# Chunked attention and a leaky-ReLU layer pair on one core: block 4's first layer in seven products, and a new order of the steps

## The chip, the cores and the metric

The kernel runs on one core of a Trainium2 chip (trn2). The metric is the device time of one execution in microseconds; of several runs the median is taken. All inputs and the output lie in HBM as fp32; the kernel computes in fp16 with fp32 sums.

## The reference

```python
# attention in chunks of 64 positions: q, k, v are (8 batches, 8 heads, 576, 64)
scores = scale * q_c @ k_c^T;  scores -= max(scores)
attn = exp(scores);  attn /= sum(attn) + 1e-9
out = attn @ v_c
# the heads side by side: x is (4608 tokens, 512)
h = x @ w_in                 # w_in  (512, 2048)
g = maximum(0.01 * h, h)
return g @ w_out             # w_out (2048, 512)
```

## The kernel before, in words

The 4608 tokens are worked through in two units. Attention goes by 36 groups of 128 tokens (two chunks of 64 for each of 8 heads); the two layers go by 19 blocks, two of 128 tokens and 17 of 256 (`BLOCKS`, line 46). Block j from 2 on consists of groups 2j-2 and 2j-1. All is in SBUF once; x of a group goes to a ring of 12 groups (`xT`, line 90).

The code emits one step after another from a list written out by hand, `ORDER` (lines 588 to 678). A step's name gives its function (`STAGES`, line 679) and its numbers; an apostrophe (`other=1`) sends it to another engine. Each engine runs its own steps in the order of the list and waits on semaphores for what it reads or overwrites. A second string, `BANKS` (line 60), names, for each tile in the order in which the steps ask for one, the PSUM bank (8 of them) or the buffer of a small ring that it gets. A tile in a bank can begin when all readers of the tile before it there are done.

For group u the steps are: `g` loads q and k (two DMAs, or four, issued by POOL), `tq`, `tk` transpose on TensorE (PE) into PSUM, with `q`, `k` copying out, or, from group 14 on, `tdq`, `tdk` transpose by a DMA issued by SP, with `cq` copying q into its padded place; `s` is the scores (8 matmuls of 64 columns), `m` the maximum and `b` the subtraction (DVE), `x` the exponential (ACT), `z` three small steps up to 1/sum, `n` the product with it (DVE, or POOL with an apostrophe), then either `e`, `c` (transpose on PE, copy) or `d` (DMA transpose from SP); `v` multiplies with v (8 matmuls of 64 columns), `a` copies x into `xT`. `L` and `vl` load v of a batch on POOL.

The layers have plain and seven-product (Strassen-like) forms.

- First layer, plain (`mm1`, line 361, step `M`): a step is 16 matmuls of 128 columns into one bank (in halves of 128 tokens, p = 1, 2, for blocks 2 to 4), and `act1` (line 386, step `G`) is the leaky ReLU on ACT from that bank to the hidden tile `gT`.
- First layer in seven products (`wide`, line 420, step `V`), from block 5 on: tokens, inputs and outputs are halved, and for each of two parts s of the outputs seven steps of 8 matmuls of 128 columns go into three banks (`xbank`, `xz`, `seed`). It needs differences of `w_in` (`w_in_sum`, line 399, step `WS`, on DVE, once), four sums of x per block (`x_sums`, line 406, step `xs`, DVE or POOL), a copy of the first product to a second bank (`wide_seed`, line 451, `ls`), a copy of the fifth to SBUF (`wide_five`, line 455, `lf`), two additions per part on DVE (`wide_add`, line 459, `la`) and four leaky ReLUs per part (`wide_leaky`, line 463, `lp`).
- Second layer: blocks 0 and 1 plain (`mm2`, line 567, step `B`, four matmuls of 512 columns, and `plain_out`, step `O`); from block 2 on seven products (`product`, line 504, step `R`, 8 matmuls of 256 columns) of sums of `gT` (`token_sums`, line 490, step `sum`, DVE) and of `w_out` (`weight_sum`, line 477, step `W`), put together by `combine` (line 551, step `comb`): 1, 6, 7 copy a partial result to SBUF, 2, 3, 5 add two into the output tile, 4 copies into it, 0 adds product 5 to a kept one.

`LATE` (line 47) lists blocks whose token halves change places in the second layer. `FIVE` (line 49) lists blocks in which products 3 and 5 have a bank each, `Z3` and `Z5`, and need `comb.0`; in the others product 3 goes on top of product 5 in one bank. `store` (line 582) writes an output tile from SP's queue. Output tiles of blocks 0 to 3 share a ring of six with the copies of `lf`; later ones have a ring of four.

## Time and profile before

| what | us |
|---|---|
| median of 3 runs (275.27 to 275.84) | 275.41 |
| the profiled execution | 275.17 |
| its span, first to last instruction | 273.0 |
| matmul busy (3909 instructions) | 264.5 |
| VectorE (DVE) busy | 235.3 |
| ScalarE (ACT) busy | 191.7 |
| GpSimd (POOL) busy | 145.4 |

The profile takes one execution, and the difference of 2.17 us between its time and its span lies before the first and after the last instruction. A row of a group shows the line, the engine, the operation, the tile written and those read, shape and count, then busy us and the mean ns of one, then idle time ahead of them and what ended it. Names of tiles: `hT` the first layer's bank when plain, `xbank`, `xz`, `seed` those of the seven products (the DVE addition at line 461 writes `xz` or `x`), `prX`, `prW`, `prZ` those of the second layer, `oP` that of the plain second layer, `SG` the sums of `gT`, `xs` the sums of x, `en` the result of `n`, `keep` and `ob` the kept results and the output tile, `QZ` q in its padded place. Matmul ends in the profile are modelled, so the rate of matmuls is read from the starts, or from runs of them in the chain.

### The profile page before, as it was taken

The page shows a single profiled execution, that of the slowest core. Times are in us where ns is not written, and L with a number is a line of the kernel's source. Part 1 is how long each engine was busy: PE and PEld are TensorE (multiplying, and loading weights), DVE is VectorE, ACT ScalarE, POOL GpSimd, SP SyncE. Part 2 cuts the span into 40 slices and gives each one's busy share as a digit, 9 for nine tenths or more (in the row PEclk, how much of TensorE's full clock was granted, in tenths as well). Part 3 has the DMA queues.
Part 4 walks back from the last instruction along what each step waited for, and adds up shares of the span by engine and source line. Part 5 has one row for each costly group of instructions (what it writes and reads, how often), then busy time and mean ns, then how long its engine had stood idle before and what let it go on. Part 6 is the DMA issues. An engine that isn't in the chain of part 4 may idle for free.

```text
span 273.0 us, 9442 instructions
## 1 busy us (share of the span) xinstructions
PE 264.5 (97%) x3909; PEld 243.6 (89%) x3909; DVE 235.3 (86%) x473; ACT 191.7 (70%) x390; POOL 145.4 (53%) x178
## 2 busy tenths in 40 slices
PE   8989999999999999997999999999999999999994
PEld 4669967999999999996999999999999999999994
DVE  7786699999989899999999999887999987687863
ACT  3767743699978988775889757789858696735330
POOL 8848386867666489591955963577163162000000
PEclk9999999999999999999999999999999999999999
DMA  9999999999999999999999999999989433102214
GB/s 141 155 190 193 206 178 156 155 123 137 139 152 155 136 178 167 131 146 156 206 142 164 186 161 147 205 145 133 89 131 162 123 103 77 43 5 75 76 43 154
DMA packets 157610, 37.96 MB, mean 139 GB/s; under 512 B 148608, under 2 KB 153088, under 8 KB 157568
## 3 DMA queue, kind: packets, MB, share of 16 engines
q0 software_dynamic: 111392, 18.10, 103.8%
q1 hardware_dynamic: 45136, 19.02, 37.9%
q8 instruction: 30, 0.49, 0.8%
q10 hardware_dynamic: 1040, 0.26, 0.4%
q14 instruction: 12, 0.10, 0.2%
HBM read 36.70 MB, written 9.44 MB: 169 GB/s over the span
## 4 chain that ended last, share of the span: by engine, by line
PE 87%; DVE 8%; ACT 2%; issue 1%; DVEq 0%
PE prX L525 20%; PE xbank L442 17%; PE prZ L525 10%; PE hT L370 10%; PE xz L442 8%; PE prW L525 5%; PE seed L442 4%; PE Sp L277 3%; PE xp L335 3%; PE oP L571 3%; PE idle L194 1%; DVE z L299 1%; PE kp L222 1%; PE qp L222 1%; ACT QZ L200 1%
## 5 line engine op out<-in xcount | busy, mean ns | idle before, releaser
L309 POOL TENSOR_TENSOR en<-ex,z 128x512 f16<-128x512 f16 x29 | 30.6, 1060 | 52.5 <-DVE z L305 35.8
L442 PEld LDWEIGHTS <-WS 128*128 128x128 f16 x896 | 54.5, 98 | 2.8 <-issue 1.0
L525 PEld LDWEIGHTS <-SG 128*128 128x128 f16 x544 | 50.9, 98 | 5.3
L442 PEld LDWEIGHTS <-w_inT 128*128 128x128 f16 x672 | 41.3, 98 | 0.5
L525 PEld LDWEIGHTS <-gT 128*128 128x128 f16 x400 | 37.2, 98 | 3.9
L117 POOL DMA_DIRECT2D q_in<-in_q_dram x39 | 33.7, 868 | 4.5 <-DMA q_in<-in_q_dram 1.3
L525 PE MATMUL prX<-TW,SG 128*128 128x256 f16 x272 | 35.2, 273 | 0.0
L442 PE MATMUL xbank<-xs,WS 128*128 128x128 f16 x448 | 33.4, 219 | 1.7 <-DVE xz L461 1.7
L117 POOL DMA_DIRECT2D k_in<-in_k_dram x39 | 32.7, 841 | 4.1 <-DMA VB<-in_v_dram 3.1
L370 PE MATMUL hT<-xT,w_inT 128*128 128x128 f16 x512 | 31.8, 219 | 0.3 <-ACT gT L384 0.3
L370 PEld LDWEIGHTS <-w_inT 128*128 128x128 f16 x512 | 29.3, 98 | 0.5 <-issue 0.4
L502 DVE TENSOR_TENSOR SG<-gT 128x1024 f16<-128x1024 f16 x34 | 25.4, 753 | 3.8 <-ACT gT L384 3.8
L284 DVE TENSOR_REDUCE mx<-Sp 128x8 f32<-128x512 f32 x36 | 24.5, 680 | 4.0 <-PE Sp L277 3.9
L200 ACT ACTIVATE xT<-xp 128x512 f16<-128x512 f32 x32 | 18.7, 595 | 11.0 <-PE xp L335 10.9
L299 DVE TENSOR_REDUCE z<-ex 128x8 f32<-128x512 f16 x36 | 24.3, 676 | 2.3 <-ACT ex L294 1.9
L122 POOL DMA_DIRECT2D VB<-in_v_dram x24 | 23.2, 981 | 4.8 <-PE xp L335 4.8
L461 DVE TENSOR_TENSOR xz<-xbank,x 128x512 f32<-128x512 f32 x28 | 19.2, 692 | 3.1 <-ACT x L200 1.9
L384 ACT ACTIVATE gT<-xz 128x512 f16<-128x512 f32 x28 | 16.5, 593 | 7.3 <-PE xz L442 7.3
L384 ACT ACTIVATE gT<-xbank 128x512 f16<-128x512 f32 x28 | 16.3, 593 | 5.6 <-PE xbank L442 3.6
L461 DVE TENSOR_TENSOR x<-xbank,x 128x512 f32<-128x512 f32 x28 | 19.0, 680 | 1.4 <-PE xbank L442 1.3
L384 ACT ACTIVATE gT<-hT 128x512 f16<-128x512 f32 x32 | 18.0, 594 | 2.2 <-PE hT L370 2.0
L200 ACT ACTIVATE keep<-prX 128x256 f32<-128x256 f32 x32 | 12.1, 384 | 10.5 <-PE prX L525 10.5
(97 smaller groups left out, 583.8 us busy)
## 6 DMA issues: line engine op xcount, KB each, us to landing
out_dram<-ob SPq DMA_DIRECT2D x35, 256.0 KB, 4.0
q_in<-in_q_dram POOLq DMA_DIRECT2D x31, 128.0 KB, 6.2
...
w_inT<-in_moe_w_in_dram POOLq DMA_DIRECT2D x8, 256.0 KB, 7.4
...
```

The source lines that it names most:

```text
L117: nc.gpsimd.dma_start(out=to, in_=rows)
L122: nc.gpsimd.dma_start(out=VB[b % NVB][m * CH:(m + 1) * CH, h0:h1, :, m * CH:(m + 1) * CH].rearrange("p h c d -> p (h c) d"), in_=v[b, m * ...
L200: nc.scalar.activation(out=to, in_=of, func=AFT.Copy, bias=0.0, scale=1.0)
L284: nc.vector.tensor_reduce(out=MX[u], in_=SP[u], axis=AXL.X, op=ALU.max)
L299: nc.vector.tensor_reduce(out=Z[u, 0], in_=EX[u], axis=AXL.X, op=ALU.add)
L309: (nc.gpsimd if other else nc.vector).tensor_tensor(out=EN[u], in0=EX[u], in1=Z[u, 2].unsqueeze(2).to_broadcast((128, 8, CH)), op=ALU.mult)
L370: nc.tensor.matmul(out=hT[:, i, :], lhsT=w_inT[:, t, fc * 128:(fc + 1) * 128], rhs=xT[:, t, r0:r0 + tb], start=(i == 0 and t == 0), stop=( ...
L384: nc.scalar.activation(out=to, in_=of, func=AFT.Prelu, bias=0.0, scale=1.0, alpha=0.01)
L442: nc.tensor.matmul(out=to[:, i, :], lhsT=left[:, t, i * 128:(i + 1) * 128], rhs=right[:, t], start=(n in (1, 5) and t == 0 and i == 0), st ...
L461: nc.vector.tensor_tensor(out=to, in0=XB[j, s], in1=X5[j, s], op=ALU.add)
L502: (nc.gpsimd if other else nc.vector).tensor_tensor(out=SG[j, n], in0=x, in1=y, op=op)
L525: nc.tensor.matmul(out=to, lhsT=left[:, f, :], rhs=right[:, f, :], start=(f == 0 and (n in (1, 2, 5) or where == "Z3")), stop=(f == HF - 1 ...
```

## The change

Block 4 leaves the lists `LATE` and `FIVE`. In the step list its eight `M4` and eight `G4` steps go, as does `comb4.0`; in their place stand fourteen `V4`, four `xs4`, two `ls4`, two `lf4`, four `la4` and eight `lp4`. From the 128th step on (group 4, block 0 in its last quarter) all steps stand in a new order, with a new `BANKS` string, and many have changed engine: over the whole list 33 `xs` are on POOL, before 29; 23 `cq` on DVE, before 15; 6 `lp` on DVE, before 2; 2 `a` on DVE, before 4; the copies of `comb`1, 4, 6 and 7 on DVE are three fewer. The 29 `n` steps on POOL stay 29. The list has 1568 steps, before 1551. The functions `load_first_v` and `cast_first_v` are new, but no step calls them, and `NV0 = 0` leaves the choice in `stage_v` as it was.

```diff
     NVB = 2
+    NV0 = 0
...
-    LATE = (2, 3, 4)
+    LATE = (2, 3)
     PLAIN = (0, 1)
-    FIVE = (2, 3, 4, 16, 17, 18)
+    FIVE = (2, 3, 16, 17, 18)
...
+    v_f = [sbp.tile([128, H // 2, 2, CH], FP32, name=f"v_f{u}", tag=f"osb4_{u + 1}") for u in range(NV0)]
...
+    def load_first_v(u):
+        for e in range(2):
+            for m in range(2):
+                c = 2 * u + e
+                nc.sync.dma_start(
...
+    def cast_first_v(u, m, other=0):
...
-                    lhsT=VB[b % NVB][:, t, c, :],
+                    lhsT=VB[1 if u < NV0 else b % NVB][:, t, c, :],
...
-        "P1 M0.2.0 z3.1 P2 z3.2 n3 M2.2.1 G0.2.0 G2.1.1 e3 M1.2.0 g6 k4 c3' G2.2.1 y5 s4 v3 M0.3.0 a3 G0.3.0 m4 M2.0.2 "
-        "G1.2.0 M2.1.2 M2.2.2 tq5 b4 x4 z4.0 WS1.0 M2.3.1 z4.1' z4.2 G2.0.2 n4' g7 q5.1 q5.0' tk5 M2.3.2 G2.1.2 L1 e4 k5' "
-        "WS2.0 s5 m5 b5 WS4.0 G2.3.1 sum2.1 x5 M1.3.0 z5.0 z5.1' z5.2 G2.3.2 c4 G1.3.0 B0.0.0 n5 B1.0.0 B1.0.1 B0.0.1 "
-        "R2.1 WS3.1 W1.0 e5 g8 B1.0.2 B1.0.3 B0.0.2 B0.0.3 sum2.2 sum2.3 comb2.1 G2.2.2 W1.1 R2.5 c5' W2.1 W2.0 O1.0 W3.1 "
-        "WS1.1 R2.6 comb2.6 O0.0 R2.2 tk7 tq7 q7.0 W4.1 W3.0 comb2.0 R2.7 tq6 tk6 sum2.4 R2.3 W4.0 k7' q7.1 comb2.7' "
-        "q6.0' g9 v5 g10 k6' s7 m7 b7 R2.4 q6.1 s6 a5 v4 g14 g11 a4 M3.0.2 M3.1.2 M3.1.1 m6 comb2.2 b6 M3.0.1 x7 G3.0.2 "
-        "x6 tq8 G3.1.1 z7.0 z7.1 M3.2.1 M3.3.1 comb2.3 z7.2 n7 comb2.5 G3.0.1 G3.1.2 q8.1' WS2.1 G3.2.1 z6.0 tk8 tq9 "
-        "M3.2.2 tk9 k8' q8.0 s8 R3.1 g12 sum3.3 e7 G3.3.1 sum3.1 sum3.2 z6.1' q9.0 z6.2 k9 q9.1 M3.3.2 comb3.1' s9 g15 "
-        "g13 comb2.4 m8 c7 R3.6 n6' G3.2.2 G3.3.2 m9 b9 comb3.6 tk10 k10 e6 tq10 R3.5 q10.1 c6' v6 tq11 st2.1 R3.7 b8 "
-        "q10.0' tdq14 x9 q11.1' s10 z9.0 a6 g17 comb3.7 tq12 m10 b10 L2 q11.0 z9.1' tk11 v7 z9.2 n9' d9 M4.1.1 tk12 R3.4 "
-        "a7 M4.2.1 x8 x10 G4.1.1 M4.1.2 k11 comb3.5 comb3.0 st0.0 s11 z8.0 k12 z8.1' M4.3.2 WS3.0 comb3.4' sum3.4 q12.1 "
-        "q12.0 z10.0 z10.1' tq13 s12 M4.3.1 WS4.1 tk13 m11 z10.2 g16 G4.1.2 z8.2 n8' G4.3.2 tdk14 q13.1 n10' b11 M4.0.2 "
-        "tdq15 M4.0.1 G4.2.1 k13' G4.3.1 q13.0 g18 x11 e8 G4.0.1 m12 b12 tdq17 z11.0 G4.0.2 z11.1' sum4.1 s13 M4.2.2 "
-        "z11.2 n11' R3.2 R4.1 R3.3 cq14.1 c8 G4.2.2 v8 d10 m13 b13 L3 x12 comb4.1 cq14.0' x13 a8 v9 comb3.2 sum4.2 R4.2 "
...
+        "P1 M0.2.0 z3.1 P2 z3.2 n3 M2.2.1 G0.2.0 G2.1.1 e3 M1.2.0 g6 k4 c3' G2.2.1 y5 s4 v3 M0.3.0 a3 M2.0.2 g7 G1.2.0 m4 "
+        "b4 M2.1.2 G0.3.0 M2.2.2 M1.3.0 M2.3.1 M2.3.2 G2.0.2 x4 G2.1.2 z4.0 WS1.0 z4.1' z4.2 WS2.0 WS3.0 n4 WS1.1 tq5 "
+        "G2.2.2 G2.3.1 L1 B1.0.0 tk5 B0.0.0 e4 WS4.0 q5.1 q5.0 k5' s5 G1.3.0 WS3.1 m5 G2.3.2 c4 sum2.1 R2.1 g9 W1.0 "
+        "B0.0.1 B1.0.1 W1.1 R2.5 B1.0.2 B1.0.3 b5 x5 g8 B0.0.2 sum2.2 z5.0 z5.1 comb2.1 O1.0 sum2.3 z5.2 W2.0 W2.1 B0.0.3 "
+        "n5 W4.1 W3.1 O0.0 R2.6 R2.2 comb2.6 g10 tq7 e5 W3.0 R2.7 q7.1 tk7 tq6 tk6 g14 comb2.0 comb2.2 sum2.4 R2.3 W4.0 "
+        "g11 c5 comb2.7 v4 k7' q7.0 s7 R2.4 k6 q6.0 WS2.1 v5 q6.1' m7 a4 g12 b7 x7 s6 M3.0.1 M3.1.1 m6 M3.2.1 comb2.4 a5 "
+        "M3.0.2 z7.0 z7.1' z7.2 G3.0.1 b6 n7 comb2.5 M3.1.2 e7 tq9 G3.1.1 x6 z6.0 comb2.3 z6.1 z6.2 g13 st2.1 M3.3.1 tk9 "
+        "G3.0.2 G3.2.1 c7' v7 G3.1.2 q9.0' n6' M3.2.2 tk8 tq8 q9.1' G3.3.1 k9' s9 a7 G3.2.2 q8.0 e6 tq10 q10.0 q10.1 "
+        "sum3.3 R3.1 comb3.1 tk10 g15 g17 sum3.1 M3.3.2 k8' q8.1' c6' xs4.1 v6 s8 k10 sum3.2 m9 G3.3.2 R3.6 tq11 a6 "
+        "V4.0.5 g16 b9 x9 m8 tk11 s10 V4.0.1 comb3.6 R3.7 q11.0 q11.1 b8 x8 ls4.0 z9.0 tq12 z9.1' xs4.2' xs4.4' L2 R3.5 "
+        "V4.0.6 V4.0.2 comb3.7 R3.4 m10 sum3.4 q12.1 lf4.0 k11' z8.0 b10 z8.1' z9.2 n9' q12.0 la4.0.3 comb3.5 z8.2 n8' "
+        "comb3.0 x10 z10.0 V4.1.1 lp4.0.2 tk12 s11 m11 b11 V4.0.3 WS4.1 tdq14 comb3.4 ls4.1 d9 k12 V4.1.5 tk13 z10.1' "
+        "lp4.0.3 V4.1.2 tdk14 st2.0 xs4.3' e8 V4.1.6 V4.0.7 z10.2 k13 tq13 R3.3 n10' lf4.1 la4.1.3 tdq17 V4.1.7 x11 z11.0 "
+        "la4.0.7 s12 g18 c8 q13.1 v8 lp4.1.2 q13.0 lp4.0.5 z11.1' la4.1.7 m12 V4.1.3 lp4.1.3 V4.0.4 lp4.0.4 s13 d10 "
+        "cq14.0' V4.1.4 lp4.1.4 lp4.1.5 tdk17 R4.1 a8 comb4.1 cq14.1' z11.2 R4.2 R3.2 v9 V5.1.1 b12 x12 m13 comb3.3 "
+        "V5.0.1 s14 sum4.1 b13 x13 sum4.2 a9 n11' xs5.1' tdq15 R4.6 comb3.2 comb4.2 ls5.0 ls5.1 m14 b14 d11 tdk15 xs5.2 "
...
-        "g": load_qk, "L": load_v, "vl": load_v_piece, "Q": load_w_in, "P": load_w_out,
+        "g": load_qk, "L": load_v, "vl": load_v_piece, "vd": load_first_v, "vf": cast_first_v, "Q": load_w_in, "P": load_w_out,
```

The steps after these, which the working below names, stand in the new list so:

```
"lp5.0.2 la5.1.3 xs5.4' V5.1.3 z13.0 g19 sum4.4 comb4.7 z14.1' z13.1' z13.2 z12.1' n13' V5.1.7 lf5.0 la5.0.3 "
...
"comb4.4 lp5.0.3 cq15.1' n12' lp5.1.5 d12 tdk18 a10 lp5.0.5 st4.1 a11 xs6.1' cq15.0' m17 comb4.3 V5.0.4 lp5.0.4 "
...
"comb9.4' ls11.1 lp11.0.3 lf11.1 V11.1.6 V11.1.2 R9.3 d22 la11.1.3 tdk26 v22 vl6.0 V11.1.7 V11.1.3 V11.0.4 "
...
"lp11.0.5 R10.5 a23 xs12.1' V12.0.1 comb10.7 R10.4 m26 b26 sum10.4 comb10.5 xs12.3' xs12.2' V12.1.5 lp11.1.4 "
...
"z27.1' ls12.1 V12.1.6 R10.3 x26 z26.0 ls12.0 V12.0.2 lp11.0.4 lf12.1 comb10.4 st8.0 tdq29 cq29.0' lp11.1.5' d24 "
...
"tdk28 s28 st9.0 R11.7 lp12.0.4 b29 x29 V12.1.4 V13.1.1 R11.5 st10.1 g32 V13.0.1 m28 b28 xs13.1' z29.0 lp12.1.5' "
...
"lp15.1.4 comb14.7 xs16.1' xs16.2' V16.1.1 comb13.3 b34 st0.0 st12.1 comb14.5 sum14.4 V16.0.1 comb14.2 R15.1 "
...
"ls16.0 z34.0 z34.1' xs16.4 z35.0 z34.2 V16.0.5 R14.3 comb14.3 lf16.0 n34' z35.1' V16.0.6 la16.0.3 R15.6 comb15.6 "
```

More of the change, by code (lines that the diff above doesn't have):

```diff
@@ L60 @@
     BANKS = (
-        "00011221230456070010314000500217016214111507112302062123352232304113201152167435233330204220335215416000300133"
-        "05714210131114622074412010011435673220555663300657700735121621342275233312370641141013315272332210000225123004"
-        "07055151026013306120334711123220154016422033022763421332653007305410112504234011560010322010022003324211212114"
-        "02506221527116304224705133112313051131306273121703373306250000060070101112133312261204414452071431011700222611"
-        "12343241623102032011016113532150531242040310212311516060077112000214331062230174302001324005012233102102345363"
-        "11240101310213241030033712103367110722000163126105303043112224400121120511031040074215622271201412521101243332"
-        "00311323370104710210220012037413003305204167002032141315061320060211173012163420102221101615122342332030133445"
-        "74012220010623230013700020104102026227351120216113104714604020412232171101133030223203510017301151207402204037"
-        "1103416073301231104153211261210142042122231402641500132020161210"
+        "00011221230456070010314000500217016214111507112302062123352232304113201152167435233330204220335253310143620000"
+        "10176517240044511551110021217166234167723700003223601102132143622201315333332220160174023540263345311207431261"
+        "54015320014070006100421101512225173164316020072301330333160732442013625700431224017154111123102261311212601202"
+        "01122235446220023131530312060700025740332213333030120020273024101261111416143105121227225501131322001740502030"
+        "21430000741113601204233333612140302303222734103102102041722213062210515610001204651123700420130232311110002427"
+        "21300110230133615301744274153102724303103401205132202121165012106221241201025521410744500421310063232735322041"
+        "33213000130721004023001370362130001210132415250312101152012121476022141503701415014200523073362041535012366403"
+        "05220110610231421211321320036223100323351300121203145210201042700021430125130003114030216100023330571711540235"
+        "1612222134140300102043001136502232700321400420102314672032012136101"
     )
@@ L328, in stage_d @@
         )
+    def load_first_v(u):
[3 more added lines that the diff above has]
+                nc.sync.dma_start(
+                    out=v_f[u][m * CH:(m + 1) * CH, :, e, :],
+                    in_=v[0, m * H // 2:(m + 1) * H // 2, c * CH:(c + 1) * CH, :].rearrange("h j d -> j h d"),
+                )
+    def cast_first_v(u, m, other=0):
+        part = slice(m * CH, (m + 1) * CH)
+        copy(other, VB[1][part, :, 2 * u:2 * u + 2, part], v_f[u][part])
     def stage_v(u):
```

134 rows, old and new, of the table ORDER are left out of this document.

## The prediction

> **What bounds the kernel now.** I read the page first, then the busy time by stretches of 10 us, then what TensorE (PE) waited for, and last the time line around its one long wait.
>
> ```profile
> span 273.0 us, 9442 instructions
> ...
> PE 264.5 (97%) x3909; PEld 243.6 (89%) x3909; DVE 235.3 (86%) x473; ACT 191.7 (70%) x390; POOL 145.4 (53%) x178
> ...
> PE 87%; DVE 8%; ACT 2%; issue 1%; DVEq 0%
> ```
>
> PE is busy for 264.5 of 273.0 us and carries 87% of the chain that ends last. The stretches say where the other 8.5 us lie (columns: stretch, its length, then busy us and instructions of PE, PEld, DVE, ACT, POOL, the granted clock, DMA):
>
> ```profile
> 0.00:10.00 10.00, 8.58 (x86) 5.21 (x86) 6.74 (x14) 4.65 (x7) 8.88 (x17) 1.00 1.52 143
> 10.00:20.00 10.00, 8.32 (x152) 6.24 (x147) 8.91 (x19) 7.01 (x12) 5.35 (x9) 1.00 1.81 180
> ...
> 30.00:40.00 10.00, 9.72 (x125) 7.74 (x125) 7.54 (x15) 5.42 (x12) 6.88 (x7) 1.00 1.56 192
> ...
> 60.00:70.00 10.00, 10.00 (x172) 9.64 (x170) 9.41 (x20) 9.41 (x22) 7.23 (x8) 1.00 2.00 140
> ...
> 120.00:130.00 10.00, 8.34 (x134) 7.68 (x132) 9.82 (x18) 4.96 (x10) 4.04 (x6) 1.00 2.12 160
> ...
> 260.00:273.00 13.00, 9.50 (x95) 8.36 (x93) 6.94 (x16) 2.08 (x6) 0.00 (x0) 1.00 0.25 90
> sum 273.00, PE 264.46 PEld 243.60 DVE 235.34 ACT 191.65 POOL 145.42; mean PE 9.79 PEld 9.02 DVE 8.72 ACT 7.10 POOL 5.39
> ```
>
> The idle time is 1.42 + 1.68 us in the start, 0.28 in 30 to 40, 1.66 in 120 to 130 and 3.50 in the last stretch, together 8.54, which is all of 273.00 - 264.46: every other stretch has PE at 10.00, at clock 1.00. So a shorter time needs either less matmul work or one of these gaps. The start (the first 127 steps of the list) is not touched, and its last eight steps are the same, so 3.1 and 3.5 us stay. Two gaps are open to a new order, 0.28 and 1.66:
>
> ```profile
> PE xbank L442 <- DVE xz L461: 1.7, 2, 0.9
> ...
> PE hT L370 <- ACT gT L384: 0.3, 1, 0.3
> ```
>
> The long one comes from a single DVE instruction:
>
> ```profile
> 118.78 0.68 DVE L502 TENSOR_TENSOR SG<-gT 128x1024 f16<-128x1024 f16 x1
> ...
> 120.51 3.10 DVE L502 TENSOR_TENSOR SG<-gT 128x1024 f16<-128x1024 f16 x1
> ...
> 120.94 2.11 POOL L309 TENSOR_TENSOR en<-ex,z 128x512 f16<-128x512 f16 x2
> ...
> 123.53 0.69 DVE L461 TENSOR_TENSOR xz<-xbank,x 128x512 f32<-128x512 f32 x1
> ...
> 124.27 0.62 PE L442 MATMUL xbank<-xs,WS 128*128 128x128 f16 x8 [0.74 <-DVE xz L461]
> ...
> 126.25 0.61 PE L442 MATMUL xbank<-xs,WS 128*128 128x128 f16 x8 [0.91 <-DVE xz L461]
> ```
>
> The same addition takes 0.68 us at 118.78 and 3.10 at 120.51, while POOL works through two `n'` steps from 120.94 to 123.05. DVE loses 2.42 us, the additions behind it (L461) come late, and PE stands for 0.74 + 0.91 = 1.65 us; so 0.77 us of the delay were covered. Three more such cases did not reach PE:
>
> ```profile
> 106.45 1.42 DVE L502 TENSOR_TENSOR SG<-SG,gT 128x1024 f16<-128x1024 f16 x1
> ```
> ```profile
> 165.02 0.98 DVE L502 TENSOR_TENSOR SG<-gT,SG 128x1024 f16<-128x1024 f16 x1
> ```
> ```profile
> 205.58 1.03 DVE L418 TENSOR_TENSOR xs<-xs,xT 128x256 f16<-128x256 f16 x1
> ```
>
> **The change part by part.** The rate of back-to-back work, from the chain and the time line:
>
> ```profile
> 33.56 0.89 PE hT L370 x16
> ...
> 35.81 3.45 PE oP L571 x16
> 39.26 0.87 PE prX L525 x8
> ...
> 110.59 1.20 DVE SG L502 x2
> ```
> ```profile
> 116.64 1.08 ACT L384 ACTIVATE gT<-xbank 128x512 f16<-128x512 f32 x2
> ```
>
> A matmul of 128 columns costs 0.89 / 16 = 0.056 us, one of 256 columns 0.87 / 8 = 0.109, a plain second-layer matmul 3.45 / 16 = 0.216. A DVE step of 512 fp32 (or 1024 fp16) elements costs 0.60 when others follow it, an ACT step 0.49 (1.08 less the 0.59 of the last one).
>
> *Matmuls.* Eight steps `M4.a.p` of 16 matmuls (128) become fourteen steps `V4.s.n` of 8 (112), all of 128 columns: 16 fewer, -0.89 us. They stood where PE is at 10.00 of 10.00, so this comes off the end as long as nothing else becomes late. The second layer of block 4 keeps its seven products; leaving LATE only swaps its halves, and leaving FIVE puts product 3 on product 5's bank and drops `comb4.0`. Product 3 must then wait for `comb4.5`; between the two lie one product and three V steps, 0.87 + 3 x 0.45 = 2.2 us of PE, for one addition of 0.4 (L556 below): nothing.
>
> *What the seven products need beside them.*
>
> ```profile
> L461 DVE TENSOR_TENSOR x<-xbank,x 128x512 f32<-128x512 f32 x28 | 19.0, 680 | 1.4 <-PE xbank L442 1.3
> ...
> L384 ACT ACTIVATE gT<-hT 128x512 f16<-128x512 f32 x32 | 18.0, 594 | 2.2 <-PE hT L370 2.0
> ...
> L200 ACT ACTIVATE seed<-xbank 128x512 f32<-128x512 f32 x23 | 13.4, 584 | 4.3 <-PE xbank L442 3.9
> ...
> L418 POOL TENSOR_TENSOR xs<-xT 128x256 f16<-128x256 f16 x14 | 9.4, 678 | 6.9 <-ACT xT L200 5.5 <-DVE xT L198 1.4
> ...
> L198 DVE COPY QZ<-QT 64x512 f16<-64x512 f16 x15 | 4.3, 284 | 0.2
> ...
> L556 DVE TENSOR_TENSOR keep<-prZ,keep 128x256 f32<-128x256 f32 x6 | 2.5, 412 | 0.0
> ```
>
> The eight `G4` and the eight `lp4` are the same ACT work (0.59 each). New are four `la4` on DVE (4 x 0.68 = 2.7 us), `ls4` and `lf4` on ACT (two each, 4 x 0.58 = 2.3), and four sums of x; over the whole list DVE keeps 27 of these and POOL gets four more (4 x 0.68 = 2.7). `comb4.0` goes (-0.41). Of the marks that choose an engine, over the whole list, steps of 512 elements to and from DVE cancel (four each way), eight `cq` go to DVE and one `q` away (7 x 0.28 = 2.0, the `q` priced alike), three short copies of products go to ACT (3 x -0.41 = -1.2, as for L556). DVE thus has 2.7 - 0.4 + 2.0 - 1.2 = 3.1 us more: 238.4 of some 272, 88% instead of 86%. None of it is on PE's path by itself; the cover is PE work, and I test that where it is thinnest.
>
> *The stretch of block 4* (in the list, from `R3.6` to `R5.1`). PE has 29.8 us of work there before and 28.4 after, counted with the rates above. ACT has 48 long steps before and 49 after, 23.5 and 24.0 us at 0.49; with the short ones I count 26.3 and 27.4. DVE has 27.9 and 27.0. So ACT goes from 88 to 96% of PE's work, and DVE is at 95%. The tightest run is from `G3.3.2` to `x12`, whose bank `V5.0.1` needs: 37 ACT steps, 29 of them long, about 16.2 us, against 17.1 us of PE. It fits with 0.8 us, less two handovers; I take nothing for it here and the excess as a rival.
>
> *A new wait.* Between `s5` and `R2.5` the new list leaves PE only `R2.1` and two `B` steps, 0.87 + 2 x 0.86 = 2.6 us, while DVE must do `m5`, `sum2.1`, `W1.0`, `W1.1`, 4 x 0.60, plus the last one's tail (0.68 - 0.60) and handovers of some 0.3 (an estimate from matmul rows that last 0.17 us beyond their rate): 2.75. PE stops for about 0.15 us; I bound it by 0 and 0.3. The old gap of 0.28 goes, since `G1.2.0` now stands ahead of `G0.3.0` on ACT.
>
> *POOL and SP.* POOL gets four more sums (33 instead of 29) beside 29 `n'` steps. `xs4.3'` stands behind `n9'` and `n8'`, and `e8` and `V4.0.7` need these soon; in block 12 `xs12.1'`, `xs12.3'`, `xs12.2'` run behind four loads of v, ahead of `V12.1.6`. Each place costs between nothing and one POOL step (0.68 to 1.06):
>
> ```profile
> L309 POOL TENSOR_TENSOR en<-ex,z 128x512 f16<-128x512 f16 x29 | 30.6, 1060 | 52.5 <-DVE z L305 35.8 <-issue 8.4 <-ACT seed L200 8.3
> ```
>
> I take 0.3 for all such places, near nothing, because PE's waits in the trace hold no POOL step. On SP's queue transposes follow each other at 1.3 us and land after about 5:
>
> ```profile
> 70.66 2.58 SPq L264 DMA_TRANSPOSE QT<-q_in  x2
> ```
> ```profile
> out_dram<-ob SPq DMA_DIRECT2D x35, 256.0 KB, 4.0
> ...
> et<-en SPq DMA_TRANSPOSE x27, 5.2
> ```
>
> The new list writes several right ahead of their reader (`tdk28` and `s28`, `d22` and `v22`), but an SP instruction starts when its queue and its source are free, and these sources (`k_in`, `en`) are there over 7 us of PE work earlier. Loads of q and k stand 21 us of PE work ahead of their DMA transposes in the middle case, 17 before. Stores moved later (`st0.0`, `st1.0`) hold their buffers longer; the next writer I find closest is `lf16.0` after `st0.0`, some 5 us of PE work, against one store of about 4. I take nothing for SP.
>
> *The delay of DVE by POOL.* Four long cases in the trace; one reached PE, for 1.65 us. The new order moves all these steps against each other. The cost is between 0 and twice 1.65; from four cases with one hit in four I expect one hit, shorter than this one, as three of the four delays (0.74, 0.3, 0.62) are under the 0.77 that was covered: 0.8.
>
> The Trainium skill, "SBUF — State Buffer", section "Who interferes with whom", states that a DVE instruction with two SBUF inputs and a GpSimd instruction that reads SBUF exclude each other for a whole instruction, and that the one issued first goes first. The rows agree on the exclusion; on the order they differ, as DVE's record begins 0.43 us before POOL's and still spans both. By that rule the delay would follow the number of POOL additions, 62 for 58, so 1.76 us instead of my 0.8, and the sum would be 1.0 us higher; it also says that an instruction with only one input in SBUF is safe, as `la4` is, and the L461 row above, mean 680 ns, agrees.
>
> *Sum*, against the profiled execution: 275.17 us (273.0 of span, 2.17 around it). 275.17 - 0.89 - 1.65 - 0.28 + 0.15 + 0.3 + 0.8 = 273.6. This execution lies 0.24 below the median of the runs, 275.41; so **273.8** as a median.
>
> **The rivals.** *ACT becomes the bound in block 4.* For: 96% of PE's work there, and steps that do not overlap take 0.59 instead of 0.49; the 29 long steps from `G3.3.2` to `x12` then need 2.9 us more, 2.1 over the slack. Against: at 60 to 70 ACT already ran at 9.41 of 10 with PE at 10.00. Price between a third of that, if only some steps fail to overlap, and all of it, 0.7 to 2.1: 274.5 to 275.9.
>
> *Slower: POOL holds DVE twice in blocks 4 and 5.* There `n9'`, `n8'`, `xs4.3'`, `n10'` and later `n13'`, `n12'`, `xs6.1'` follow each other on POOL, beside `sum3.4` and `sum4.1` to `sum4.4` on DVE, and DVE at 95% cannot catch up. Price: two delays of 2.42 with one cover of 0.77, 4.1 us of PE waits. Without any wait the time would be 275.41 - 0.89 - 1.65 - 0.28 = 272.6; so 276.7. It decides the sign once PE's waits after the start exceed 2.8 us, and shows as slower from 3.4. This is the mechanism of the page named above. For: the pairs in the list; against: only one of four delays reached PE.
>
> *The saving is given back.* The 16 matmuls go in any case, but the gap at 120 may return elsewhere, whole, and the new waits come at their upper bounds, 0.3 at `R2.5` and one POOL sum of 0.68: 272.6 + 1.65 + 0.98 = 275.2, no change. For: DVE at 88%, as full as before; against: each of these bounds would have to be met at once.
>
> **How the numbers follow.** A run of this kernel can tell about 0.2%, 0.55 us, from no change: faster is below 274.86, slower above 275.96. My forecast (PE's waits 0 to 2 us, 272.6 to 274.6): 0.53. ACT as the bound: 0.17, half of it under 274.86. No change: 0.13. Slower: 0.17. So faster 0.53 + 0.09 = 0.62, same 0.08 + 0.13 = 0.21, slower 0.17. The range starts at 272.6, no wait at all, and reaches into the slower case to 276.0, leaving out most of that case and little else.
>
> **What would show it.** 3893 matmuls instead of 3909. PE at 10.00 in the stretch of 120 to 130. A wait of `prZ` (L525) for DVE near 40 us, 0.1 to 0.3. No ACT wait ahead of PE near 80 us. DVE busy about 239 us. SG additions over 1 us show the delay by POOL, and PE's waits of `xbank` or `prX` behind them its price. I would be wrong if PE's waits after 35 us add up to more than 2 us, or if the time falls while they don't.

## The result, and the profile after

| | before | after |
|---|---|---|
| median of 5 runs each, us | 275.41 (275.02 to 276.21) | 273.99 (273.44 to 274.38) |
| ratio, with its 95% interval | | 0.9943 (0.992 to 0.9965) |
| the profiled execution, us | 275.17 | 273.44 |
| its span, us | 273.0 | 271.7 |
| matmuls | 3909 | 3893 |

The change makes the kernel faster by 1.4 us, 0.57%, against a forecast of 273.8 (272.6 to 276.0). First the head of the page of the changed kernel and its chain:

```profile
span 271.7 us, 9412 instructions
...
PE 262.8 (97%) x3893; PEld 242.0 (89%) x3893; DVE 235.5 (87%) x481; ACT 189.8 (70%) x389; POOL 148.0 (54%) x182
...
PE 84%; DVE 10%; ACT 3%; issue 1%; POOL 1%; DVEq 0%; POOLq 0%
```

The stretches of 10 us, with the columns of before (stretch, length, PE, PEld, DVE, ACT, POOL, clock, DMA):

```profile
0.00:10.00 10.00, 7.89 (x88) 4.64 (x89) 6.74 (x14) 4.88 (x7) 8.88 (x17) 1.00 1.63 148
10.00:20.00 10.00, 8.33 (x151) 6.33 (x150) 8.90 (x19) 7.01 (x12) 5.86 (x10) 1.00 1.80 178
...
30.00:40.00 10.00, 10.00 (x127) 7.96 (x125) 8.56 (x16) 5.38 (x11) 4.05 (x4) 1.00 1.58 191
...
60.00:70.00 10.00, 10.00 (x168) 9.63 (x166) 9.75 (x20) 9.90 (x24) 8.56 (x10) 1.00 2.44 141
70.00:80.00 10.00, 10.00 (x156) 9.47 (x154) 9.64 (x21) 9.45 (x20) 5.07 (x6) 1.00 1.65 145
...
90.00:100.00 10.00, 9.83 (x144) 9.07 (x143) 10.00 (x23) 9.19 (x20) 7.79 (x10) 1.00 1.97 146
100.00:110.00 10.00, 9.44 (x143) 8.82 (x141) 8.84 (x17) 7.64 (x16) 5.84 (x7) 1.00 1.85 167
...
120.00:130.00 10.00, 10.00 (x160) 9.57 (x159) 9.92 (x24) 6.88 (x15) 5.81 (x7) 1.00 1.99 144
...
260.00:271.70 11.70, 7.30 (x75) 6.38 (x73) 6.27 (x17) 0.00 (x0) 0.00 (x0) 0.97 0.26 91
```

The gap of 1.66 us at 120 to 130 is gone, and so is the one of 0.28 at 30 to 40. In block 4 (60 to 90) PE has no gap, though ACT is at 9.90 of 10 where it had 9.41. Two new gaps stand at 90 to 110, 0.17 + 0.56 us, and the last stretch has 4.40 us without PE where it had 3.50. What PE waited for after 34 us:

```profile
PE seed L457 <- DVE seed L200: 0.6, 1, 0.6
PE xbank L457 <- DVE xs L433: 0.2, 1, 0.2
```

The time line around the larger wait, with POOL's and DVE's rows:

```profile
103.22 0.69 DVE L517 TENSOR_TENSOR SG<-gT 128x1024 f16<-128x1024 f16 x1
103.83 1.13 DVE L433 TENSOR_TENSOR xs<-xs,xT 128x256 f16<-128x256 f16 x1
103.86 0.89 POOL L118 DMA_DIRECT2D k_in<-in_k_dram  x1
104.76 1.09 POOL L311 TENSOR_TENSOR en<-ex,z 128x512 f16<-128x512 f16 x1
104.88 1.52 DVE L517 TENSOR_TENSOR SG<-SG,gT 128x1024 f16<-128x1024 f16 x1
...
106.33 0.69 DVE L200 COPY seed<-xbank 128x512 f32<-128x512 f32 x1
...
107.06 0.61 PE L457 MATMUL seed<-xT,w_inT 128*128 128x128 f16 x8 [0.56 <-DVE seed L200]
```

It is the old mechanism at a new place. POOL's `n17'` (104.76) holds the token sum beside it, 1.52 us for 0.69. The sum of x ahead of it is slow as well (1.13 us; the same form takes 0.28 below), while POOL only issues a load. DVE thus comes to the copy `ls7.0'` 1.7 us late (0.83 + 0.85), and PE waits for it.

A finer account than the idle time takes the start of each matmul in the trace and subtracts its usual distance from the one before (0.056, 0.109, 0.216 us by kind); what is left is a wait. Summed by stretch, in us:

| | before | after | difference | forecast |
|---|---|---|---|---|
| matmuls at their usual distance | 262.78 | 261.89 | -0.89 | -0.89 |
| waits up to 30 us | 3.15 | 2.47 | -0.68 | -0.28 |
| 30 to 60 | -0.03 | 0.14 | +0.17 | +0.15 |
| 60 to 90 | -0.01 | -0.01 | 0 | 0 |
| 90 to 115 | -0.01 | 1.27 | +1.28 | +0.3 and +0.8 |
| 115 to 135 | 1.98 | -0.01 | -1.99 | -1.65 |
| 135 to the last matmul | 0.03 | -0.04 | -0.07 | 0 |
| last matmul to the end | 3.81 | 4.64 | +0.83 | 0 |
| time outside the span | 2.13 | 1.76 | -0.37 | 0 |

The differences inside the span add up to -1.35, and the span fell from 273.04 to 271.68 (the 1.3 us ahead of the first matmul, in no row, are the same in both). Of the -0.68 up to 30 us, 0.44 is the old gap at 30 us, counted from start to start. The rest depends on when the first loads land: over all profiled runs of this study the waits up to 30 us lie between 2.47 and 3.65, and the changed kernel's 2.47 is the lowest of them (2.91 to 3.65 in the other kernels with its order), so some of this trace's gain is luck. The time outside the span is not: its median over the runs is 2.09 to 2.12 us in the kernels with as many VectorE instructions as before (567) and 1.76 to 1.79 in those with as many as the changed kernel (578) or more.

### The profile page after: what moved, and what is told of

The parts are those of the page before. It is cut to its first block, busy times and chain, and to the rows that moved or that the text cites. A ratio compares the mean times of both kernels' runs of the same rounds, so it can differ in the third digit from the quotient of the medians.

```text
span 271.7 us, 9412 instructions
## 1 busy us (share of the span) xinstructions
PE 262.8 (97%) x3893; PEld 242.0 (89%) x3893; DVE 235.5 (87%) x481; ACT 189.8 (70%) x389; POOL 148.0 (54%) x182
## 4 chain that ended last, share of the span: by engine, by line
PE 84%; DVE 10%; ACT 3%; issue 1%; POOL 1%; DVEq 0%; POOLq 0%
PE prX L540 20%; PE xbank L457 18%; PE prZ L540 10%; PE xz L457 9%; PE hT L385 7%; PE prW L540 5%; PE seed L457 4%; PE xp L350 3%; PE Sp L279 3%; PE oP L586 3%; DVE SG L517 1%; ACT QZ L202 1%; DVE mx L286 1%; DVE z L301 1%; DVE xs L433 1%
## 5 line engine op out<-in xcount | busy, mean ns | idle before, releaser
L457 PEld LDWEIGHTS <-WS 128*128 128x128 f16 x960 | 58.1, 98 | 1.0 <-DVE xs L433 0.3
L457 PEld LDWEIGHTS <-w_inT 128*128 128x128 f16 x720 | 44.9, 98 | 1.5 <-issue 0.7
L457 PE MATMUL xbank<-xs,WS 128*128 128x128 f16 x480 | 35.1, 219 | 0.2 <-DVE xs L433 0.2
L202 ACT ACTIVATE xT<-xp 128x512 f16<-128x512 f32 x34 | 20.0, 596 | 9.4 <-PE xp L350 9.4
L476 DVE TENSOR_TENSOR xz<-xbank,x 128x512 f32<-128x512 f32 x30 | 20.6, 694 | 5.6 <-ACT x L202 2.4
L517 DVE TENSOR_TENSOR SG<-gT 128x1024 f16<-128x1024 f16 x34 | 23.8, 708 | 0.1
L385 PE MATMUL hT<-xT,w_inT 128*128 128x128 f16 x384 | 23.1, 219 | 0.0
L399 ACT ACTIVATE gT<-seed 128x512 f16<-128x512 f32 x30 | 17.8, 594 | 7.5 <-PE seed L457 7.2
L385 PEld LDWEIGHTS <-w_inT 128*128 128x128 f16 x384 | 21.8, 98 | 0.1
L476 DVE TENSOR_TENSOR x<-xbank,x 128x512 f32<-128x512 f32 x30 | 20.3, 679 | 1.1 <-PE xbank L457 0.9
L433 POOL TENSOR_TENSOR xs<-xT 128x256 f16<-128x256 f16 x16 | 10.8, 682 | 19.0 <-ACT xT L202 17.5
```

The lines of the kernel that those rows point to most:

```text
L202: nc.scalar.activation(out=to, in_=of, func=AFT.Copy, bias=0.0, scale=1.0)
L385: nc.tensor.matmul(out=hT[:, i, :], lhsT=w_inT[:, t, fc * 128:(fc + 1) * 128], rhs=xT[:, t, r0:r0 + tb], start=(i == 0 and t == 0), stop=( ...
L399: nc.scalar.activation(out=to, in_=of, func=AFT.Prelu, bias=0.0, scale=1.0, alpha=0.01)
L457: nc.tensor.matmul(out=to[:, i, :], lhsT=left[:, t, i * 128:(i + 1) * 128], rhs=right[:, t], start=(n in (1, 5) and t == 0 and i == 0), st ...
L476: nc.vector.tensor_tensor(out=to, in0=XB[j, s], in1=X5[j, s], op=ALU.add)
L517: (nc.gpsimd if other else nc.vector).tensor_tensor(out=SG[j, n], in0=x, in1=y, op=op)
```

## The experiments

Each was timed in alternation with the kernel before on the same chip; ratios are to that one. The first four shared one chip.

### sum7_later: the old stall by itself

The kernel before, with one step moved two places down its list:

```diff
-z18.2 comb6.3 sum7.3 la8.0.3 z20.0 tdq21
+z18.2 comb6.3 la8.0.3 z20.0 sum7.3 tdq21
```

> The kernel before, with one step moved: the third sum of block 7's hidden tile stands two places later on DVE, behind the addition and the row sum that stood behind it. In the trace of before this sum was the instruction of 3.10 us, while POOL did two n steps. Theory (the delay of DVE by POOL costs the kernel before its 1.65 us at 123 us, because the addition that PE waits for stands behind the sum): the sum may still be held, but the addition is done, and 1.0 to 1.65 us go: 273.8 to 274.4. Rival (another DVE step with two inputs in SBUF is held instead, or PE meets the next late step): 275.1 to 275.7, no change.

Measured: 273.81 us (before there 275.17), ratio 0.995 (0.9929 to 0.9972), 1.36 us less. Time line and wait:

```profile
120.78 0.70 DVE L461 TENSOR_TENSOR xz<-xbank,x 128x512 f32<-128x512 f32 x1 [0.17 <-PE xbank L442]
120.97 2.09 POOL L309 TENSOR_TENSOR en<-ex,z 128x512 f16<-128x512 f16 x2
121.39 0.68 DVE L299 TENSOR_REDUCE z<-ex 128x8 f32<-128x512 f16 x1
121.98 1.64 DVE L502 TENSOR_TENSOR SG<-gT 128x1024 f16<-128x1024 f16 x1
...
125.08 0.61 PE L442 MATMUL xbank<-xs,WS 128*128 128x128 f16 x8 [0.64 <-DVE xz L461]
```

The addition `la8.0.3` and a reduction, which POOL doesn't hold, now run beside the first `n'`, and the sum meets only the second: 1.64 us instead of 3.10. One wait of 0.64 is left of two of 0.74 and 0.91. From start to start, 0.80 us is left of 1.98. So a move of one step gets nearly all that the whole change got. The change's own parts must cancel for the most part, and the other runs say which.

### after_again, plain4 and twice4: what the seven products are worth

`after_again` is the changed kernel, unchanged, on this chip. `plain4` keeps its order and gives block 4 the plain form back: eight `M4` and `G4` steps in place of `V4`, `xs4`, `ls4`, `lf4`, `la4`, `lp4`. `twice4` does the first product of block 4 twice:

```diff
-        for i in range(4):
+        for i in 2 * list(range(4)) if (j, n) == (4, 1) else range(4):
```

> The changed kernel once more. If PE's waits are set by the order, the two waits of its first trace, 0.2 us at 93 us and 0.6 us at 107 us, stand again at the same steps, and the last stretch again has 4.4 us without matmuls; if they come by chance, they stand elsewhere and the last stretch is nearer to the 3.5 us of the kernel before. The time: 273.4 to 274.4 either way.

> The changed kernel's order with block 4's first layer in the plain form again: eight steps of 16 matmuls stand at eight of the fourteen places of the seven products, eight leaky ReLUs in place of the others, and the sums, copies and additions that only the seven products need are gone. The rest of the order is the changed kernel's. Theory (PE's work is the bound also in block 4, so the 16 matmuls count in full): 16 x 0.056 = 0.89 us slower than the changed kernel's 273.99, so 274.9, less up to 0.3 because DVE and ACT each lose four steps; PE's waits after the start stay near 0.8 us. Rival (the new order alone made the gain, the 16 matmuls lay beside ACT and DVE at 95% and were hidden): 274.0, no difference from the changed kernel.

> The changed kernel, with the first product of block 4's first layer done twice into the same bank, for both parts of the outputs: 16 matmuls of 128 columns more, nothing else moved. Theory (PE is the bound in this stretch): +0.89 us against the changed kernel's 273.99, so 274.9. Rival (ACT or DVE at 95% of PE's work is the bound there): PE has idle time to give, +0 to 0.3, so 274.0 to 274.3.

| | us | ratio (interval) |
|---|---|---|
| after_again | 273.56 (273.45 to 276.31) | 0.9948 (0.9926 to 0.997) |
| plain4 | 273.86 (273.64 to 274.83) | 0.9946 (0.993 to 0.9963) |
| twice4 | 274.46 (274.36 to 276.83) | 0.9977 (0.9953 to 1.0) |

Sixteen matmuls more in block 4 cost 0.90 us in `twice4`, all of their 0.89: PE sets the pace there, with the seven products too. But `plain4`, which also has sixteen more, loses only 0.30, nearer to its rival's 0 than to the theory's 0.9. Its trace has the same waits as the changed kernel (30 to 60: 0.14 us, 90 to 115: 1.28) and the same 0.89 of matmuls more. What differs is the end: from the last matmul to the end it takes 3.80 us, as before, and not 4.64; 0.20 of that comes back outside the span (median 1.98 us, in `after_again` 1.78). So the saving is there, and 0.64 of it is lost at the end: 0.89 - 0.64 = 0.25, against the 0.30 measured. Both `after_again` and `twice4` have the longer end as well (4.64, 4.65).

### tail_fetch and fetch_before: the longer end

The page counts the packets by queue. The row of queue 14 (kind, packets, MB, share) is in before and after:

```profile
q14 instruction: 12, 0.10, 0.2%
```
```profile
q14 instruction: 13, 0.11, 0.1%
```

These are reads of program code in the course of the run, 8192 bytes each. In the trace's records of single packets, two of the last come at VectorE's 448th and at its 575th instruction. The kernel before has 567 VectorE instructions, `plain4` 571, the changed kernel 578 (all its instructions, those that don't count as busy too). So only the changed kernel reaches the 575th, at 269.3 us, while its last outputs are being stored. (In `plain4` the read falls after the end of the span.) If that is the cause, more VectorE instructions early on should cure it, and a few more in the kernel before should bring it there. `tail_fetch`, from the changed kernel, and `fetch_before`, from the one before:

```diff
+    spare = sbp.tile([128, 1], FP16, name="spare")
+    def pad(n):
+        for _ in range(n):
+            nc.vector.memset(spare, 0.0)
...
-V17.1.2 comb15.4' ls17.0
+V17.1.2 comb15.4' pad24 ls17.0
```
```diff
-V17.1.1 comb15.6' ls17.1'
+V17.1.1 comb15.6' pad11 ls17.1'
```

> The changed kernel with 24 memsets of one column put on VectorE near 234 us, where it waits 2.27 us for an evacuation; nothing else is changed. Theory: the 0.9 us by which the end after the last product grew (from its start to the end of the span 3.77 us before, 4.67 after) is a 13th read of program code, due when VectorE has reached about its 575th instruction, which then falls between the last stores. With 24 more instructions ahead it is read near 257 us, the end takes 3.8 us again, and the time falls by 0.7 to 0.9, to 272.8 (ratio to before 0.9915). Rival: the longer end comes of the order of the last stores, or by chance; then the time stays at 273.6 (ratio 0.994) and the end at 4.6 us. A loss would mean that the memsets hold a step of VectorE.

> The mirror of tail_fetch, on the kernel before: 11 memsets of one column are added on VectorE ahead of ls17.1', where it waits 1.43 us, so that VectorE has 578 instructions as the changed kernel has, and not 567. Theory: VectorE's fifth read of code, which the kernel before never reached, now falls between the last stores; the end grows from 3.8 to 4.6 us and the time by 0.7 to 0.9, to 275.9 (ratio to before 1.003). Rival: the longer end belongs to the new order of stores and copies, and tail_fetch gained by chance; then the end stays at 3.8 us and the time at 275.1 (ratio 1.000).

| | us | ratio (interval) | VectorE instructions | read at | last matmul to end |
|---|---|---|---|---|---|
| tail_fetch | 273.04 (272.83 to 273.19) | 0.9903 (0.9866 to 0.9941) | 602 | 256.2 us | 3.81 us |
| fetch_before | 276.74 (275.82 to 277.88) | 1.0053 (1.0024 to 1.0082) | 578 | 271.7 us | 4.94 us |

The last eight matmuls and the span, of before (its span is 273.0 us), after, `tail_fetch` and `fetch_before` in turn:

```profile
268.46 1.04 PE L525 MATMUL prW<-w_outT,gT 128*128 128x256 f16 x8
```
```profile
span 271.7 us, 9412 instructions
...
266.27 1.04 PE L540 MATMUL prW<-w_outT,gT 128*128 128x256 f16 x8
```
```profile
span 271.3 us, 9436 instructions
...
266.73 1.04 PE L546 MATMUL prW<-w_outT,gT 128*128 128x256 f16 x8
```
```profile
span 274.1 us, 9453 instructions
...
268.36 1.04 PE L531 MATMUL prW<-w_outT,gT 128*128 128x256 f16 x8
```

From the start of this group to the end it is 4.6, 5.4, 4.6 and 5.7 us. Both directions came out: 24 instructions that do nothing made the changed kernel faster (0.5 us against the median of `after_again` on another chip, 1.2 by the two ratios, whose intervals overlap), and 11 made the kernel before slower, by 0.0053 x 275.29 = 1.5 us, more than the 0.9 expected. The runs of `fetch_before` scatter from 275.82 to 277.88; lowest run against lowest run (274.89) it is 0.93, and its trace has 1.13 at the end, less 0.3 outside the span. So the reads of code, by the number of VectorE's instructions, decide on the length of the end. The order of the last stores, the rival, is the same in `fetch_before` and before. Nor does any read at the end do it: the changed kernel's other late read, at 267.1 us, stands in `tail_fetch` too (267.5), where the end is short.

How one read of 8 KB holds the end shows in the trace's records of packets and landings. The last store lands in 16 parts, and the end waits for all of them. In us from the start of the last matmul:

| | before | tail_fetch | after | fetch_before |
|---|---|---|---|---|
| VectorE's last read of code | long over | long over | 2.29 to 2.65 | 2.60 to 2.91 |
| 15 parts of the last store have landed | 2.82 | 2.80 | 2.83 | 2.85 |
| the sixteenth part | 2.85 | 2.82 | 3.65 | 3.95 |

In the changed kernel a packet of the store begins in the moment in which the read ends, 2.65, and three more follow it without a gap (2.73, 2.95, 3.17), when all other packets of the store have begun by 2.47. So one part of sixteen waits behind the read. (The records do not name the engine that moved a packet; that it is one queue is read from the times.)

A longer end is not all loss. Outside the span the kernels with 567 VectorE instructions spend 2.09 to 2.12 us in the median, `plain4` with 571 spends 1.98, and those with 578 or more 1.76 to 1.79, `tail_fetch` among them. So the late read costs the changed kernel 0.83 - 0.33 = 0.5 us net, and `tail_fetch`, whose read comes early, has the short end and the short time outside. Why the time outside falls is open.

With equal ends, `tail_fetch` and `plain4` compare the two forms of block 4: each against its own kernel before, 275.04 - 273.04 = 2.00 and 275.17 - 273.86 = 1.31, so 0.69 us, of which 0.20 lies outside the span. On two chips this is too rough to tell 0.5 from 0.9; the matmul account (0.89) and `twice4` (0.90, on one chip with `after_again`) are the better measures.

### n17_later: the new wait at 107 us

`n17'` goes behind the loads of `g23`, and its transpose with it:

```diff
-xs8.1 n17' d17 a14 lp7.1.5 g23 R6.5
+xs8.1 a14 lp7.1.5 g23 n17' d17 R6.5
```

> The changed kernel with GpSimd's n17' moved behind the loads of g23 (and the transpose d17 behind it), no more. Theory: the wait of 0.56 us at 107 us comes of VectorE's token sum (1.52 instead of 0.69 us), held by this n17'; without it TensorE waits 0 to 0.1 there and the time falls by 0.4 to 0.6, to 273.1 (ratio to before 0.9925). Second theory: GpSimd's issue of a load, too, holds an addition of two operands from SBUF that began just before it; then the sum, now beside the issues of g23, still takes over 1 us, and 0.2 to 0.5 of the wait is left. Rival: the wait is made by the order on TensorE and not by GpSimd; nothing changes.

Measured: 273.07 us (272.76 to 274.27; before there 275.04), ratio 0.9913 (0.988 to 0.9945), some 0.5 us under the changed kernel. The same steps in its trace, then a wait that is new:

```profile
104.69 0.28 DVE L433 TENSOR_TENSOR xs<-xs,xT 128x256 f16<-128x256 f16 x1
104.89 0.69 DVE L517 TENSOR_TENSOR SG<-SG,gT 128x1024 f16<-128x1024 f16 x1
105.50 0.69 DVE L200 COPY seed<-xbank 128x512 f32<-128x512 f32 x1
...
107.50 1.10 DVE L433 TENSOR_TENSOR xs<-xT,xs 128x256 f16<-128x256 f16 x1
```
```profile
126.50 0.41 PE L350 MATMUL xp<-et,VB 128*128 128x64 f16 x8 [0.49 <-DMA et<-en]
```

With `n17'` gone the sum takes 0.69 and the sum of x 0.28, though POOL issues loads beside both; the second theory fails. The wait at 107 is gone, and `n17'` now holds another sum at 107.50, where it harms nobody. The later transpose costs 0.49 at 126: in this execution most of what was freed is given back (waits at 90 to 115 fall from 1.28 to 0.55, those at 115 to 135 come to 0.66). It is the longest of the seven, 274.27; whether the transpose came in time in the other runs (the median of all seven is 1.2 us lower), no trace shows.

### port and port2: what on POOL holds an addition on DVE

Two kernels by themselves, with streams of equal instructions on both engines. In `port` both operands of the sum are the same tile, in `port2` they differ.

> A kernel of its own, which computes nothing of the reference: seven stretches of 12 equal VectorE instructions each. Additions of two 128x1024 operands from SBUF: alone, beside 8 issues of loads by GpSimd, beside 7 multiplications by GpSimd; additions of PSUM and SBUF (128x512) beside issues and beside multiplications; copies of PSUM beside both. Theory: both kinds of GpSimd work hold the additions from SBUF alone: alone 0.6 us from start to start, some beside issues 0.9 to 1.5, beside multiplications most over 1.0; with an operand from PSUM none is held. Rival by the Trainium skill's SBUF page: the multiplications hold them, the issues don't (all 0.6). Rival: what was held in the kernel was held by something else; all are 0.6.

> A kernel of its own, which computes nothing of the reference: additions of two different f16 operands from SBUF, written in turn to two tiles as in the kernel's pipeline, 40 of 128x1024 and 90 of 128x256 beside 28 issues of loads by GpSimd and beside 20 multiplications; 40 of 128x1024 beside a mix (two issues, one multiplication); 40 additions of PSUM and SBUF beside each. In port, 12 sums beside 8 issues took 0.72 us each, as alone, beside 7 multiplications 1.14. Theory: issues hold such additions now and then (in the kernel about one in ten of those that met one), so some 4 of 40 take over 0.9 us, and 3 to 9 of the 90 short ones over 0.5; beside multiplications about half or more are held. Rival: issues alone hold none, and what the kernel showed comes only where a multiplication stands near: then the mix shows holds next to issues and the first two stretches none.

In `port` 12 sums took 8.68 us alone (0.72 each, not the 0.6 expected) and 8.68 beside 8 issues, and 13.73 beside 7 multiplications; additions of PSUM and SBUF and copies of PSUM took 8.66 beside either. `port2` by its seven stretches (columns as above, without PE; DVE's and POOL's instruction counts in brackets):

```profile
4.90:29.00 24.10, 24.10 (x42) 0.00 (x0) 24.10 (x29) 1.00 2.23 131
30.40:48.60 18.20, 18.20 (x91) 0.00 (x0) 18.01 (x22) 1.00 2.33 141
56.20:97.10 40.90, 40.90 (x41) 0.00 (x0) 28.64 (x22) 1.00 0.14 7
98.00:133.00 35.00, 35.00 (x91) 0.00 (x0) 24.09 (x22) 1.00 0.00 0
134.00:170.60 36.60, 36.60 (x41) 0.00 (x0) 27.27 (x29) 1.00 1.01 65
173.60:197.40 23.80, 23.80 (x41) 0.00 (x0) 23.52 (x28) 1.00 2.08 130
199.40:223.20 23.80, 23.80 (x41) 0.00 (x0) 21.21 (x22) 1.00 0.25 12
```

Issues alone hold nothing: 40 sums in 24.1 us, 0.60 each, and 90 short ones in 18.2, 0.20 each, the rates of the kernel. Beside 20 multiplications the 40 take 40.9 us and the 90 take 35.0; in each stretch 20 sums are slow, one for each multiplication, at 1.52 and 1.13 us. Additions with an operand in PSUM take 23.8 beside either. So for these streams the theory that issues hold a sum now and then falls, and the rival is right, in the mix as well. There (fifth stretch, 10 of 40 sums slow) two rows of sums with POOL's rows around them:

```profile
134.62 1.83 POOL L64 DMA_DIRECT2D qt<-in_q_dram  x2
135.16 1.53 DVE L56 TENSOR_TENSOR C<-A,B 128x1024 f16<-128x1024 f16 x1
```
```profile
139.95 0.87 POOL L64 DMA_DIRECT2D qt<-in_q_dram  x1 [0.53 <-DMA qt<-in_q_dram]
140.47 1.99 DVE L56 TENSOR_TENSOR C<-A,B 128x1024 f16<-128x1024 f16 x1
140.84 1.05 POOL L68 TENSOR_TENSOR F<-E,pg 128x512 f16<-128x512 f16 x1
```

The first sum is over at 136.69; it is slow while POOL still issues the load (to 136.45) behind which the multiplication is next. The second began 0.37 us ahead of the multiplication and yet lasts until 142.46, past the multiplication's end at 141.89. So, by the records, a multiplication can hold a sum that began before it, and one during the issue ahead of it. Of the ten slow sums in the mix the first alone is of the second kind; the other nine end some 0.55 us after their multiplication, as do the 20 of the third stretch. This is what the rows of 103.83 and 104.88 in the changed kernel show (the second ends at 106.40, 0.55 after `n17'`), and with `n17'` moved both went.

The Trainium skill, "SBUF — State Buffer", section "Who interferes with whom", states that a DVE instruction with two SBUF inputs and a GpSimd instruction that reads SBUF exclude each other, infers that descriptor generation does not hold a `tensor_tensor`, and states that whoever issues first goes first. `port2` agrees on the first two. On the third the records differ in the mix, where nine of the ten slow sums begin before their multiplication does, but not in the third stretch, where each of the 20 multiplications begins 0.39 us before the sum that it holds. Starts on POOL are rough in these profiles, so which of the two had issued first in the mix is not shown.

Of the ten slow sums of before and after, seven overlap a POOL addition or multiplication. The other three (1.16, 1.13 and 1.05 us at 80.13, 91.61 and 118.00 in after) stand beside issues of loads and are over 0.5 us or more before POOL's next addition or multiplication begins; what holds these stays open.

### act_more: the rival that ACT is the bound

Three of ACT's evacuations in block 4 are done twice:

```diff
-V4.1.1 lp4.0.2 tk12
+V4.1.1 lp4.0.2 lp4.0.2 tk12
...
-z10.1' lp4.0.3 V4.1.2
+z10.1' lp4.0.3 lp4.0.3 V4.1.2
...
-v8 lp4.1.2 q13.0
+v8 lp4.1.2 lp4.1.2 q13.0
```

> The changed kernel with three steps of ScalarE in block 4 done twice (lp4.0.2, lp4.0.3, lp4.1.2: the same evacuation again, same result), 3 x 0.49 us more on ScalarE between 66 and 82 us. By the ledger of the two engines, ScalarE is 0.8 us ahead of what TensorE asks of it there: if it is that close to being the bound, 1.47 us more costs 0.5 to 0.9 us (274.3, ratio to before 0.996). Rival: ScalarE's busy time overstates its work, it has over 1.5 us of room, and the time stays within 0.2 us (273.6, ratio 0.9945). Other rival: it was the bound already, and all 1.5 us come out (275.1, ratio 0.999).

Measured: 275.63 us (275.4 to 276.82), ratio 1.0012 (0.999 to 1.0033), so 0.0064 x 275 = 1.8 us more than the changed kernel. The stretch and two of the waits:

```profile
70.00:80.00 10.00, 8.86 (x134) 7.93 (x133) 7.77 (x17) 9.90 (x22) 4.23 (x5) 1.00 1.55 152
```
```profile
PE Sp L279 <- ACT QZ L202: 0.6, 1, 0.6
...
PE qp L224 <- ACT KT L202: 0.4, 1, 0.4
```

All 1.47 us come out, and 0.4 more (PE's waits at 60 to 90 rise from 0 to 1.91 us). Nothing is left of the 0.8 us of room in the ledger. The waits arise at attention steps, `s13` and `tq13`, whose copies stand behind the evacuations in ACT's queue. With `twice4` this says that in block 4 PE and ACT are both full, at least at these places: more of either costs its whole price. The three steps were added ahead of copies that PE soon needs; the same work elsewhere in the block was not tried. The plain form left room: in `plain4` ACT is busy 26.41 us of 60 to 90, in the changed kernel 28.40.

### three_edits: the faster version

The changed kernel with the memsets, `n17'` where POOL was idle, and one sum of x ahead of a token sum:

```diff
-V17.1.2 comb15.4' ls17.0
+V17.1.2 comb15.4' pad24 ls17.0
...
-R5.3 comb5.3 a13 xs7.1' d15
+R5.3 comb5.3 a13 n17' xs7.1' d15
...
-xs8.1 n17' d17 a14
+xs8.1 d17 a14
...
-V6.1.5 sum5.1 xs6.2 comb5.1'
+V6.1.5 xs6.2 sum5.1 comb5.1'
```

> The changed kernel with three edits: the 24 memsets of tail_fetch; n17' moved ahead of xs7.1', where GpSimd stands idle for 1.77 us (in n17_later it went behind the loads, and its transpose then came 0.5 us late for the product v17 at 125 us); xs6.2 moved ahead of sum5.1 on VectorE, so that it starts at 91.0 and not at 91.6 us, when a load is issued. Theory: the three gains lie at different places of TensorE's chain and add up: 0.8 (end) + 0.6 (107 us) + 0.3 to 0.5 (93 and 96 us), 271.9 (ratio to before 0.988); the trace shows no wait of TensorE over 0.1 us after 47 us. Rival: each wait that goes gives way to one behind it, as in n17_later, and only the end's 0.8 and some 0.3 are kept, 272.5 (0.9905). Slower than tail_fetch (273.0): n17' or sum5.1 in its new place holds something that TensorE needs.

Measured: 272.01 us (271.63 to 273.32; before there 275.06), ratio 0.987 (0.9832 to 0.9908). The stretches that had the gaps, with the last one:

```profile
90.00:100.00 10.00, 10.00 (x145) 9.33 (x142) 10.00 (x23) 9.71 (x22) 7.95 (x10) 1.00 1.90 158
100.00:110.00 10.00, 10.00 (x156) 9.54 (x154) 8.27 (x19) 8.18 (x17) 6.35 (x8) 1.00 1.88 168
...
260.00:270.60 10.60, 7.11 (x73) 6.21 (x71) 6.07 (x17) 0.00 (x0) 0.00 (x0) 1.00 0.28 100
```

The gains add up as the theory had it: PE is at 10.00 in both stretches, the waits from 90 to 115 are 0.22 us instead of 1.28, and the last stretch has 3.49 us without PE. One wait over 0.1 us is left against the theory, 0.15 at 96.6, behind a token sum that is slow now (1.19 us at 93.00). This version beats the changed kernel by 1.6 us and the kernel before by 3.1.

## Why the prediction came out as it did

The time was right, and the two largest terms of the sum were, in cause and nearly in size. That it came within 0.2 us is partly luck, since errors of about 1 us in either direction cancel in it. The longer end (+0.83), and new waits that were 0.2 more than the forecast, stand against the gap at 120 (0.34 more than taken), the first 30 us (0.40 more) and the time outside the span (0.37), which the sum kept at 2.17.

- **Matmuls, -0.89.** Right: -0.89 in the account and 0.90 in `twice4`.
- **The gap at 120, -1.65, and the one at 30, -0.28.** Right in cause. The first was worth a little more, 1.99: start to start, each wait also costs the handover that the wait's own row leaves out. The second was worth 0.44 for the same reason; the other 0.24 of the first 30 us lies within the scatter of the first loads.
- **A new wait at `R2.5`, +0.15.** Wrong place, and right in size by luck: no wait stands at `prZ` near 40 us, and one of 0.16 at `prX` at 45.8.
- **Delays of DVE by POOL, +0.8, and places on POOL, +0.3.** The first was right in mechanism and size: "one hit, shorter than this one" was 0.73 us at 107 (0.56 in the waits), and it went with `n17'`. The second did not come: no wait of PE there is for a POOL step. The rest of the 1.28 us at 90 to 115 is 0.34 and 0.15 behind a slow sum of x at 91.61. The first of these went when `three_edits` moved that sum; what made it slow is open. Where the slower rival expected two hits, beside `sum3.4` and `sum4.1` to `sum4.4` (60 to 90 us), PE waited for nothing.
- **Block 4 at no cost.** Right, by no margin. The prediction gave ACT 0.8 us of room and took the excess as a rival; `act_more` shows no room at the places that it tried. The rival did not happen, but the prediction's count of ACT's work left too much room.
- **"The start ... and its last eight steps are the same, so 3.1 and 3.5 us stay."** This is the step that failed. The same last steps took 0.83 us longer, since what decides on them is also how many instructions VectorE has had before (578 for 567, so that a read of code fell among the last stores). The step counted work and order, and not the code. The same holds for the 2.17 us around the span, which it kept and which fell by 0.37.
- **What would show it.** 3893 matmuls, 10.00 at 120 to 130, no ACT wait near 80 and slow `SG` rows came out. DVE busy was to be about 239 us and is 235.5. The steps themselves were counted right: the durations of DVE's rows add up to 261.6 us before and 263.6 after, and the excess of the slow sums among them fell from 4.4 to 3.4, so without it they grew by 3.1 us, as forecast. But rows that follow each other overlap, by 26.2 us in all before and 28.1 after, and busy time counts an overlap once. A step priced at the 0.68 us of its row adds only 0.60 to a busy stretch.

That the change won is due, for the most part, to the order: `sum7_later` gets 1.36 us by moving one step, and the seven products with the rest of the new order added 0.25 to that. Against `sum7_later`, the products' 0.89, the gap at 30 (0.44), the last 0.80 of the old stall and 0.31 outside the span stand for the change; 1.28 of new waits at 90 to 115, 0.17 before them and 0.82 at the end stand against it (2.4 and 2.3 us).
